# Attention, soft mixture and MLP in one kernel: keys and queries of most pairs loaded further ahead, one buffer cleared by VectorE, fewer filling products

## The chip, the cores and the metric

The kernel runs on one core of a Trainium2 chip (trn2). The metric is device time of one execution in microseconds (us): the median of the runs, which for the kernel before is 782.35 us.

## What is computed

Three stages in a row, all in float32 in the reference:

```python
q_pool = q.reshape(B, H, S // 2, 2, D).mean(axis=3)        # 4 x 8 x 576 x 64
scores = q_pool @ k.T / sqrt(D);  scores -= scores.max(-1)   # 576 queries x 1152 keys
x = softmax(scores) @ v                                      # then (B * 576) x 512 tokens
logits = x @ phi;  d = softmax over tokens;  slots = d.T @ x # 8 experts x 4 slots
slot_out[e] = relu(slots[e] @ w1[e]) @ w2[e]
x = softmax over slots (logits) @ slot_out
h = x @ w_in;  g = h where h >= 1, 0 where h <= -1, else (h + 1)^2 / 4
out = g @ w_out
```

q, k and v are 4 x 8 x 1152 x 64. The change touches the first stage alone, and the way the work is laid out there.

## The kernel before

**Pairs, steps, slots.** The 32 heads are taken as 16 pairs P = 0..15. The keys of a pair are cut into 9 chunks of 128, so a pair takes 9 steps, and step g = 9 P + c works on chunk c of pair P. A step has two slots h = 0, 1, one for each head. Below, (g, h) names a slot; negative steps are the start-up. In a slot TensorE computes, in this order: products whose maxima belong to a pair 11 steps ahead (`max_half`, L305; VectorE reduces them, L317), the transposed scores of this chunk (`st`, L371: four products with the keys K and then four with a second operand S, which hold the low parts of K and q and the subtracted maximum), and the products of the exponentials of the chunk before with V (`pv`, L401). ScalarE takes the exponential of the scores (L376), and VectorE adds exponentials for the denominators (L384). PSUM tiles of products and scores come from one pool of three buffers.

**Preparing a pair.** Keys and queries are split into two 16-bit floats (high and low part) and transposed by DMA. For pair P the steps are: load K and q (`load_k2`, L229, two DMAs; `load_q`, L237 to L240, four DMAs), high part of K on ScalarE (`prep_khi`, L252), low part on VectorE (`prep_klo`, L260), sum of neighbouring queries (`prep_qp`, L273), its high part (`prep_qhi`, L276), its low part (`prep_qlo`, L283), transposition of K in two halves (`xpose_k`, L266) and of the high part of q (`xpose_q1`, L288), a copy of the transposed q into the other 64 partitions (`dup_q1`, L291), and, when all maxima of the pair are there, `max_fin` with the transposition of the low part of q and the maxima (q2, L354). `s2_fill` (L294) copies K into S, `load_v` (L246) loads V.

**What sets the order.** The order is written out by hand. `at(g, h, f, ...)` puts a function into a slot, and `plan(P)` does so for a pair with offsets from the row of `PREP` (L44) that L587 picks: its entries are the step of the loads, of `prep_khi`, the half-steps of `prep_klo`, the half-step of `prep_qp`, the step of `prep_qhi` and the half-step of `prep_qlo`. Pair 2 takes the first row, pairs 3 to 15 the second. Pairs 0 and 1 are prepared by code of their own at the start, where POOL takes over some of the work for pair 1 (the scaling L679 among it). Each engine runs its instructions in program order. All DMAs are issued by SyncE's queue (SP), in program order too: a row that waits holds all rows behind it. The tiles `kf` and `qf` of the loads are single buffers, so the loads of a pair wait until `prep_klo` and `prep_qlo` of the pair before have read them.

**Between the loads** SP also issues rows of a background conversion: an output write (L209) and a load (L185) of weights.

**Start.** L663 to L665 clear the unused parts of qn2 and S, once for each of two buffers. `fill(FILL[2])` (L337) issues 128x128 products on the identity that nobody reads, 11 of them in slot (-3, 1); each is a float32 product and shows as two matrix rows.

**LGT** (L33) holds the half-steps at which the logits of a batch, and what follows from them, are put (`lg_part` to `p_add`).

Of the kernel before, what the change touches and what calls it, by code (L numbers as in the profile page):

```python
# [17 lines left out]


WARM = 2, 2, 3, 2, 4, 3  # L20
FILL = 28, 0, 11

AHEAD = 2
RUN = 3
# [5 lines left out]
P1G = -2, -1, 0, 1, 2, 3, 4, 5, 6  # L30
TMUL = (12, 0, 0, (0, 1)), (12, 1, 0, (2,)), (12, 1, 1, (0,)), (13, 0, 1, (1, 2))
TXN = 0, 1
LGT = 30, 31, 32, 33, 34, 36, 37  # L33
LPT = 6
WPH = 3
REA = 0
# [4 lines left out]
ADD = ((4, 1, 0, 0, 2), (5, 1, 1, 0, 1), (6, 1, 1, 1, 2), (6, 2, 0, 0, 2), (7, 2, 1, 0, 2), (8, 3, 0, 0, 1), (9, 3, 0, 1, 2),  # L41
       (10, 3, 1, 0, 2), (10, 4, 0, 0, 1), (11, 4, 0, 1, 2), (12, 4, 1, 0, 1), (13, 4, 1, 1, 2))

PREP = (-20, -18, (-34, -33), -36, -16, -30), (-24, -22, (-41, -37), -41, -19, -37)  # L44


@with_exitstack
def fused_kernel(ctx: ExitStack, tc: tile.TileContext, q, k, v, phi, w1, w2, w_in, w_out, out):
    nc = tc.nc
    B, H, S, D = q.shape  # L50
# [113 lines left out]
    S2b = [pr_p[i].tile([128, 2 * NK, 128], F16, name=f"S2_{i}") for i in range(2)]  # L164
    qn2b = [g2.tile([128, NK, 128], F16, name=f"qn2_{i}") for i in range(2)]
# [57 lines left out]
    def load_k(P, h):  # L223
        b, hp = divmod(P, HPB)
        if h == 0:

            kft[P] = g0.tile([128, 2, NK, D], F32, tag="kf", name=f"kf{P}") if P != 1 else \
                xT[:, 0:2].rearrange("p h (c d) -> p h c d", c=NK)
        nc.sync.dma_start(out=kft[P][:, h], in_=k[b, 2 * hp + h].rearrange("(p c) d -> p c d", p=128))  # L229
# [66 lines left out]
    def max_half(P, t, a):  # L296
# [10 lines left out]
        if P == 0:  # L307
            fill(FILL[1])
        rt = RT[P] if P < len(RT) else ()
# [23 lines left out]
    def fill(n):  # L333
        if not fl:
            fl[0] = acc_tile(0, "fill")
        for _ in range(n):
            nc.tensor.matmul(fl[0][:, 0:128], lhsT=ident, rhs=ident, start=True, stop=True)  # L337
# [243 lines left out]
    def at(g, slot, f, *a):  # L581
        sched.setdefault((g, slot), []).append((f, a))

    def plan(P):
        b = NK * P
        if P > 1:
            lk, hk, lok, aq, hq_, loq = PREP[P > 2]  # L587
            for h in range(2):
                at(b + lk, 0, (load_k2, load_q)[h], P)
                at(b + hk, h, prep_khi, P, h)  # L590
                at(b + lok[h] // 2, lok[h] % 2, prep_klo, P, h)
                at(b - 17, h, xpose_k, P, h)
            at(b + aq // 2, aq % 2, prep_qp, P)
            at(b + hq_, 0, prep_qhi, P)
            at(b - 16, 0, xpose_q1, P)
            at(b + loq // 2, loq % 2, prep_qlo, P)
            at(b - 15, 1, dup_q1, P)
        if P > 0:
            at(b - 8, 1, load_v, P)
            at(b - 9 if P > 1 else 1, 1, s2_fill, P)  # L600
        for s, *a in ADD:
            at(b + s // 2, s % 2, es_add, P, *a)
        for h in range(2):
            at(b + 9, h, tail_raw, P, h)
            if h and P:
                at(b + 2, 0, tail_fin, P - 1)
            at(b + 9, h, tail_sum, P, h)
        for c, i, ns in TAT:
            pre[b + c, i] = P, ns
        last = P == NP - 1  # L610
        if not last:
            at(b + 11, REA, tail_rec, P)
        for i in range(2):
            at(b + (10 if last else 12), i if last else TXN[i], tail_xn, P, i)
            if last:
                at(b + 12, i, tail_mul, P, i)
        if not last:
            for c, sl, *a in TMUL:
                at(b + c, sl, tail_mul, P, *a)
        if last:  # L620
            at(b + 11, 0, tail_rec, P)
            at(b + 11, 0, tail_fin, P)
        at(b + 13 + (not last), last, tail_xt, P)
        if P % HPB == HPB - 1:
            q_ = P // HPB
            if last:
                at(b + LPT, 1, lg_part, q_)
                at(b + 11, 1, lg_half, q_)
                at(b + 14, 1, lg_sum, q_)
                at(b + 14, 1, warm, WARM[0])  # L630
                at(b + 14, 1, raw_mm, range(B - 1))
                at(b + 14, 1, warm, WARM[5])
                at(b + 15, 1, lg_max, q_)
                at(b + 15, 1, lg_exp, q_)
                at(b + 15, 1, lg_raw, q_)
                at(b + 16, 1, lg_nat, q_)
                at(b + 16, 1, warm, WARM[1])
                at(b + 18, 1, raw_mm, (B - 1,))
                at(b + 18, 1, warm, WARM[2])
                at(b + 17, 0, p_mm, q_)  # L640
                at(b + 17, 0, p_add, q_)
            else:
                for f, t in zip((lg_part, lg_sum, lg_max, lg_exp, lg_nat, p_mm, p_add), LGT):
                    at(b + t // 2, t % 2, f, q_)
# [9 lines left out]
    with tc.manual_schedule():  # L654
# [4 lines left out]
        load_k(1, 1)  # L659
        fill(FILL[0])  # L660
        for i in range(2):
            eng = nc.gpsimd if i else nc.vector
            eng.memset(qn2b[i][:, :, D:2 * D], 0.0)  # L663
            eng.memset(S2b[i][64:128], 0.0)
            nc.gpsimd.memset(S2b[i][64:65], MS)  # L665
        prep_khi(0, 0)
        prep_klo(0, 0)
# [18 lines left out]
        for (g, i), *f in R1:  # L686
            for x in f:
                at(g, i, *x)
        at(-3, 1, fill, FILL[2])
        at(-3, 1, prep_qlo, 1)  # L690
        at(-2, 1, cv_load, 0)
        at(-2, 1, cv_load, 1)
        at(-2, 1, cv_load, 2)
# [1 line left out]
        for P in range(NP):  # L695
            plan(P)
# [8 lines left out]
        for g in range(-LEAD, nsteps + 1):  # L705
            mx = [divmod(g + LEAD, NK)] if not NK <= g + LEAD < 2 * NK else []
            mx += [(1, t) for t in range(NK) if P1G[t] == g]
            P, c = divmod(g, NK)
# [425 lines left out]
```

## Time and profile before

| what | value |
|---|---|
| median of 3 runs | 782.35 us (782.05 to 782.71) |
| profiled execution, its own time | 787.7 us |
| its span | 785.9 us |
| mean granted TensorE clock | 0.983 of full |
| TensorE (PE) busy | 757.1 us, 96% |
| VectorE (DVE) busy | 581.4 us, 74% |
| ScalarE (ACT) busy | 451.7 us, 57% |
| GpSimd (POOL) busy | 125.9 us, 16% |

The span runs from the first to the last instruction of the profiled execution. Busy time is the union of an engine's instructions. A share of 96% on PE is an average over stages: the start-up and a few places behind it are where PE stands still or runs at half clock. "Granted clock" is the share of TensorE's full clock that the chip lets through; 1.00 is 2.4 GHz and 0.50 is 1.2 GHz.

### The profile page before, as it was taken

What the parts mean: (1) busy time and instruction counts of PE and PEld (TensorE: products, weight loads), DVE (VectorE), ACT (ScalarE), POOL (GpSimd) and SP (SyncE); (2) the same over time, 40 slices, a digit from 0 to 9 for tenths busy, and PEclk for the clock granted to TensorE, in tenths of its full rate; (3) what the DMA queues carried; (4) which work ended last, traced back from release to release, by engine and by line L of the source; (5) the groups of instructions that cost most, each with busy time, mean ns of one, the idle gap of its engine ahead of it and who ended that gap; (6) DMA issues with size and microseconds to landing.
All of it is one profiled execution on the core that took longest, in us unless ns stands there. A gap on an engine that the chain in (4) does not pass through costs nothing.

```text
span 785.9 us, 19049 instructions
## 1 busy us (share of the span) xinstructions
PE 757.1 (96%) x7896; PEld 556.6 (71%) x7896; DVE 581.4 (74%) x947; ACT 451.7 (57%) x855; POOL 125.9 (16%) x100
## 2 busy tenths in 40 slices
PE   7779999999999999999999999999789999999998
PEld 6557777766767766777766776633578888888887
DVE  6878999988989888999988793151697777666520
ACT  4246667676657565676675666401686777556620
POOL 7000000000000000000000000002574444443330
PEclk8889999999999999999999999999989999999999
DMA  8786788797788797799998836799600000000000
GB/s 215 201 174 137 182 193 205 206 248 200 186 233 203 183 260 164 188 263 180 212 263 134 222 96 237 269 333 395 241 0 28 28 28 20 7 28 28 27 28 28
DMA packets 138263, 127.11 MB, mean 162 GB/s; under 512 B 80576, under 2 KB 100288, under 8 KB 137408
## 3 DMA queue, kind: packets, MB, share of 16 engines
q1 hardware_dynamic: 138176, 125.89, 61.0%
q8 instruction: 62, 1.02, 0.6%
q14 instruction: 25, 0.20, 0.1%
HBM read 87.10 MB, written 13.11 MB: 128 GB/s over the span
## 4 chain that ended last, share of the span: by engine, by line
PE 60%; DMA 2%; DVE 2%; ACT 2%; issue 1%; SPq 0%; ACTq 0%; DVEq 0%
PE acc L401 9%; PE st L371 9%; PE po L1031 8%; PE po L1032 8%; PE po L1033 8%; PE mx L305 4%; PE acc L394 3%; DMA wi<-wi_dr 2%; PE h L968 2%; PE h L775 2%; PE tx L439 1%; PE tb L466 1%; DVE r L1021 1%; PE tr L428 1%; PE lp L482 0%
## 5 line engine op out<-in xcount | busy, mean ns | idle before, releaser
L376 ACT ACTIVATE e<-st 128x576 f32<-128x576 f32 x288 | 187.0, 651 | 139.0 <-PE st L371 125.6
L317 DVE TENSOR_REDUCE mp<-mx 128x1 f32<-128x576 f32 x282 | 212.1, 754 | 44.9 <-PE mx L305 38.0
L401 PE MATMUL acc<-e,vf 128*64 128x288 f32 x1152 | 195.1, 411 | 0.5 <-ACT e L376 0.5
L305 PE MATMUL mx<-K,q 128*64 128x288 f16 x1152 | 124.8, 298 | 9.6 <-DVE mp L317 3.4
L371 PE MATMUL st<-q,K 128*64 128x288 f16 x1152 | 122.0, 288 | 5.9 <-ACT e L376 4.7
L371 PE MATMUL st<-q,S 128*64 128x288 f16 x1152 | 122.0, 287 | 0.0
L305 PEld LDWEIGHTS <-q 128*64 128x64 f16 x1152 | 66.3, 112 | 70.2 <-issue 24.5
L1031 PE MATMUL po<-whi,ghi 128*128 128x512 f32 (+1 forms) x280 | 108.5, 388 | 0.0
L1032 PE MATMUL po<-wlo,ghi 128*128 128x512 f32 (+1 forms) x280 | 108.5, 388 | 0.0
L1033 PE MATMUL po<-whi,glo 128*128 128x512 f32 (+1 forms) x280 | 108.0, 386 | 0.0
L981 DVE TENSOR_TENSOR r<-cl,r 128x1024 f32<-128x1024 f32 x34 | 80.6, 2372 | 36.9 <-ACT cl L980 36.9
L987 POOL TENSOR_TENSOR glo<-r,ghi 128x1024 fp32r<-128x1024 f32 x34 | 82.2, 2417 | 95.3 <-ACT ghi L986 95.3
L401 PEld LDWEIGHTS acc<-e,vf 128*64 128x64 f32 x1152 | 77.4, 137 | 8.3 <-ACT e L376 2.0
L371 PEld LDWEIGHTS <-K 128*64 128x64 f16 x1152 | 68.3, 110 | 20.9 <-issue 12.7
L752 POOL MEMSET xfer<- 128x1024 f32 x1 | 1.0, 957 | 493.5 <-PE pb L562 493.5
L384 DVE TENSOR_TENSOR es<-es,e 128x288 f32<-128x288 f32 (+1 forms) x144 | 77.5, 550 | 2.2 <-ACT e L376 2.2
L371 PEld LDWEIGHTS <-S 128*64 128x64 f16 x1152 | 69.3, 110 | 3.4
L971 ACT ACTIVATE r<-h,cols 128x512 f32<-128x512 f32 x68 | 43.0, 685 | 31.4 <-PE h L968 31.4
L1033 PEld LDWEIGHTS po<-whi,glo 128*128 128x128 f32 x280 | 53.2, 190 | 10.8
L1031 PEld LDWEIGHTS po<-whi,ghi 128*128 128x128 f32 x280 | 53.4, 191 | 9.8
L1032 PEld LDWEIGHTS po<-wlo,ghi 128*128 128x128 f32 x280 | 53.3, 190 | 9.3
L972 DVE TENSOR_SCALAR cl<-h 128x512 f32<-128x512 f32 x68 | 43.8, 685 | 15.8 <-ACT r L971 13.9
(191 smaller groups left out, 854.1 us busy)
## 6 DMA issues: line engine op xcount, KB each, us to landing
w<-in_moe_w_dram SPq DMA_DIRECT2D x31, 1024.0 KB, 7.9
vf<-in_v_dram SPq DMA_DIRECT2D x16, 576.0 KB, 6.1
kf<-in_k_dram SPq DMA_DIRECT2D x30, 288.0 KB, 4.1
f<-in_moe_w_out_dram SPq DMA_DIRECT2D x16, 512.0 KB, 5.1
f<-in_moe_w_in_dram SPq DMA_DIRECT2D x16, 512.0 KB, 5.5
qf<-in_q_dram SPq DMA_DIRECT2D x30, 256.0 KB, 4.9
S<-K SPq DMA_DIRECT2D x16, 288.0 KB, 5.6
out_dram<-ob SPq DMA_DIRECT2D x17, 256.0 KB, 2.0
```

Source lines behind the costliest of these rows:

```text
L305: nc.tensor.matmul(ps[p0:p1, i, 0:HQ], lhsT=q1[P][:, t, p0:p1], rhs=kk[:, j * HQ:(j + 1) * HQ], start=True, stop=True)
L317: nc.vector.tensor_reduce(out=mp[P][:, t, a:a + 1], in_=ps[:, :, 0:HQ], op=ALU.max, axis=AX.XY)
L371: nc.tensor.matmul(ps[c0:c0 + 64, i, 0:HQ], lhsT=kk[:, ci, c0:c0 + 64], rhs=f[:, sl[i]], start=first, stop=not first)
L376: nc.scalar.activation(out=e, in_=ps[:, :, 0:HQ], func=AF.Exp, scale=ESC)
L384: nc.vector.tensor_tensor(out=Es[P, n, h][:, i0:i1], in0=a[:, i0:i1], in1=b[:, i0:i1], op=ALU.add)
L401: nc.tensor.matmul(acc[P, i][h * 64:(h + 1) * 64, 0:HQ], lhsT=vt[P][:, h, c, :], rhs=E[P, c, h][:, i, :], start=(c == 0), stop=(c == NK - ...
L972: nc.vector.tensor_scalar(out=cl[:, a:b], in0=src, scalar1=-1.0, scalar2=1.0, op0=ALU.max, op1=ALU.min)
L981: nc.vector.tensor_tensor(out=r[:, sl], in0=cl[:, sl], in1=r[:, sl], op=ALU.add)
L987: nc.gpsimd.tensor_tensor(out=glo[n, qd][:, sl], in0=r[:, sl], in1=ghi[n, qd][:, sl].bitcast(F32), op=ALU.subtract)
L1031: nc.tensor.matmul(po, lhsT=ghi[n, qd][:, j, sl], rhs=whi[:, f, cs], start=(f == 0), stop=False)
L1032: nc.tensor.matmul(po, lhsT=ghi[n, qd][:, j, sl], rhs=wlo[:, f, cs], start=False, stop=False)
L1033: nc.tensor.matmul(po, lhsT=glo[n, qd][:, j, sl], rhs=whi[:, f, cs], start=False, stop=(f == 15))
```

## The change

- `FILL[2]` goes from 11 to 3: 6 matrix rows in place of 22.
- The clearing of the second S buffer (64 partitions of S) moves from POOL to VectorE, which clears it as 1152 elements of 32 bits instead of 2304 of 16.
- `prep_qlo(1)` moves from slot (-3, 1) to (-1, 1).
- The first row of `PREP` now holds for pairs 2 and 3, the second for pairs 4 to 15. Pair 3 so loads at step 7 instead of 3 and its four VectorE operations stand at half-steps 18, 20, 21 and 24 instead of 13, 13, 17 and 17.
- In the second row the loads come two steps earlier (-26 instead of -24).
- For pairs 4 to 15 the transpositions of K and q and the copy of q come one step earlier.
- The last three entries of `LGT` come one slot later (34, 36, 37 become 35, 37, 38).

```diff
--- before.py
+++ after.py
@@ -18,7 +18,7 @@
 
 
 WARM = 2, 2, 3, 2, 4, 3
-FILL = 28, 0, 11
+FILL = 28, 0, 3
 
 AHEAD = 2
 RUN = 3
@@ -30,7 +30,7 @@
 P1G = -2, -1, 0, 1, 2, 3, 4, 5, 6
 TMUL = (12, 0, 0, (0, 1)), (12, 1, 0, (2,)), (12, 1, 1, (0,)), (13, 0, 1, (1, 2))
 TXN = 0, 1
-LGT = 30, 31, 32, 33, 34, 36, 37
+LGT = 30, 31, 32, 33, 35, 37, 38
 LPT = 6
 WPH = 3
 REA = 0
@@ -41,7 +41,7 @@
 ADD = ((4, 1, 0, 0, 2), (5, 1, 1, 0, 1), (6, 1, 1, 1, 2), (6, 2, 0, 0, 2), (7, 2, 1, 0, 2), (8, 3, 0, 0, 1), (9, 3, 0, 1, 2),
        (10, 3, 1, 0, 2), (10, 4, 0, 0, 1), (11, 4, 0, 1, 2), (12, 4, 1, 0, 1), (13, 4, 1, 1, 2))
 
-PREP = (-20, -18, (-34, -33), -36, -16, -30), (-24, -22, (-41, -37), -41, -19, -37)
+PREP = (-20, -18, (-34, -33), -36, -16, -30), (-26, -22, (-41, -37), -41, -19, -37)
 
 
 @with_exitstack
@@ -584,17 +584,17 @@
     def plan(P):
         b = NK * P
         if P > 1:
-            lk, hk, lok, aq, hq_, loq = PREP[P > 2]
+            lk, hk, lok, aq, hq_, loq = PREP[P > 3]
             for h in range(2):
                 at(b + lk, 0, (load_k2, load_q)[h], P)
                 at(b + hk, h, prep_khi, P, h)
                 at(b + lok[h] // 2, lok[h] % 2, prep_klo, P, h)
-                at(b - 17, h, xpose_k, P, h)
+                at(b - 17 - (P > 3), h, xpose_k, P, h)
             at(b + aq // 2, aq % 2, prep_qp, P)
             at(b + hq_, 0, prep_qhi, P)
-            at(b - 16, 0, xpose_q1, P)
+            at(b - 16 - (P > 3), 0, xpose_q1, P)
             at(b + loq // 2, loq % 2, prep_qlo, P)
-            at(b - 15, 1, dup_q1, P)
+            at(b - 15 - (P > 3), 1, dup_q1, P)
         if P > 0:
             at(b - 8, 1, load_v, P)
             at(b - 9 if P > 1 else 1, 1, s2_fill, P)
@@ -659,9 +659,8 @@
         load_k(1, 1)
         fill(FILL[0])
         for i in range(2):
-            eng = nc.gpsimd if i else nc.vector
-            eng.memset(qn2b[i][:, :, D:2 * D], 0.0)
-            eng.memset(S2b[i][64:128], 0.0)
+            (nc.gpsimd if i else nc.vector).memset(qn2b[i][:, :, D:2 * D], 0.0)
+            nc.vector.memset(S2b[i][64:128], 0.0)
             nc.gpsimd.memset(S2b[i][64:65], MS)
         prep_khi(0, 0)
         prep_klo(0, 0)
@@ -687,7 +686,7 @@
             for x in f:
                 at(g, i, *x)
         at(-3, 1, fill, FILL[2])
-        at(-3, 1, prep_qlo, 1)
+        at(-1, 1, prep_qlo, 1)
         at(-2, 1, cv_load, 0)
         at(-2, 1, cv_load, 1)
         at(-2, 1, cv_load, 2)
```

**SP between the transposition of pair 2's K and pair 1's q2.** K1_P, q1_P and q2_P are the transposed tiles of pair P, kfP and qfP its loads, phs is the weight phi. Before:

```order
L288 DMA_TRANSPOSE q1_2_478<-qn1_105 128x9x128
L229 DMA kf3_523<-in_k_dram 128x576 x2
L237 DMA qf3_526<-in_q_dram 128x4x128
L238 DMA qf3_526<-in_q_dram 128x4x128
L239 DMA qf3_526<-in_q_dram 64x128
L240 DMA qf3_526<-in_q_dram 64x128
L291 DMA q1_2_478<-q1_2_478 64x1152
L694 DMA phs_100<-in_moe_phi_dram 128x4x32
L354 DMA_TRANSPOSE q2_1_666<-qn2_1_104 128x9x128
```

After the change:

```order
L288 DMA_TRANSPOSE q1_2_470<-qn1_105 128x9x128
L291 DMA q1_2_470<-q1_2_470 64x1152
L693 DMA phs_100<-in_moe_phi_dram 128x4x32
L354 DMA_TRANSPOSE q2_1_647<-qn2_1_104 128x9x128
L229 DMA kf3_709<-in_k_dram 128x576 x2
L237 DMA qf3_712<-in_q_dram 128x4x128
L238 DMA qf3_712<-in_q_dram 128x4x128
L239 DMA qf3_712<-in_q_dram 64x128
L240 DMA qf3_712<-in_q_dram 64x128
```

The loads of pair 3 now stand behind the copy of q1_2, the load of phi and the transposition of q2_1, where they stood ahead of them.

**SP around the transposition of pair 3's q.** vf2 is V of pair 2; wo_dr and f64 are the background conversion. Before:

```order
L266 DMA_TRANSPOSE K1_3_881<-kn3_614 128x9x128
L246 DMA vf2_904<-in_v_dram 128x2x576
L266 DMA_TRANSPOSE K1_3_881<-kn3_614 128x9x128
L209 DMA wo_dr_74<-wst1_797 128x512
L185 DMA f64_4_909<-in_moe2_w_out_dram 128x1024
L288 DMA_TRANSPOSE q1_3_939<-qn1_105 128x9x128
L229 DMA kf4_991<-in_k_dram 128x576 x2
L237 DMA qf4_994<-in_q_dram 128x4x128
L238 DMA qf4_994<-in_q_dram 128x4x128
L239 DMA qf4_994<-in_q_dram 64x128
L240 DMA qf4_994<-in_q_dram 64x128
L291 DMA q1_3_939<-q1_3_939 64x1152
```

After the change:

```order
L266 DMA_TRANSPOSE K1_3_870<-kn3_821 128x9x128
L229 DMA kf4_872<-in_k_dram 128x576 x2
L237 DMA qf4_875<-in_q_dram 128x4x128
L238 DMA qf4_875<-in_q_dram 128x4x128
L239 DMA qf4_875<-in_q_dram 64x128
L240 DMA qf4_875<-in_q_dram 64x128
L246 DMA vf2_901<-in_v_dram 128x2x576
L266 DMA_TRANSPOSE K1_3_870<-kn3_821 128x9x128
L209 DMA wo_dr_74<-wst1_781 128x512
L185 DMA f64_4_907<-in_moe2_w_out_dram 128x1024
L288 DMA_TRANSPOSE q1_3_938<-qn1_105 128x9x128
L291 DMA q1_3_938<-q1_3_938 64x1152
```

The six loads of pair 4 now stand ahead of the second half of K1_3 and of the transposition of q1_3, which they followed.

**VectorE in step 12, where the low part of pair 3's q now stands** (es0 and es1 are sums of exponentials, mp2 the maxima of pair 2). After the change:

```order
L317 TENSOR_REDUCE mp2_665<-mx2_5_0_961 128x1
L384 TENSOR_TENSOR es1_0_1_959<-e1_0_1_840,e1_1_1_896 128x288
L384 TENSOR_TENSOR es1_0_0_932<-es1_0_0_932,e1_2_0_924 128x576
L283 SCALAR_TENSOR_TENSOR qn2_1_104<-qf3_712,qn1_105 128x9x64
L317 TENSOR_REDUCE mp2_665<-mx2_5_1_993 128x1
L384 TENSOR_TENSOR es1_0_1_959<-es1_0_1_959,e1_2_1_955 128x576
```

L283 for pair 3, which reads qf3, stood in step 8, and now stands behind the sums of step 12; the loads of qf4 into the same buffer wait for it.

## Rows read from the trace of the kernel before

**Rows 1.** Windows: stretch, its length, busy us (instructions) of PE, PEld, DVE, ACT, POOL, granted clock, DMA share, GB/s.

```profile
22.60:29.00 6.40, 5.59 (x29) 4.72 (x27) 5.14 (x12) 0.00 (x0) 0.00 (x0) 0.50 0.52 99
53.00:59.60 6.60, 5.57 (x40) 3.56 (x41) 3.89 (x8) 2.90 (x5) 0.00 (x0) 0.50 0.35 67
```

**Rows 2.** Timeline of the start: start us, us, engine, line, operation, [idle before, releaser].

```profile
1.44 1.02 DVE L664 MEMSET S<- 64x1152 uint32 x1 [0.28 <-issue]
...
4.08 0.91 SPq L229 DMA_DIRECT2D xT<-in_k_dram  x2
4.57 0.76 DVE L260 SCALAR_TENSOR_TENSOR kn<-kf,kn 128x576 f16<-128x576 f32 x1 [2.11 <-ACT kn L252]
...
7.37 2.01 POOL L665 MEMSET S<- 1x2304 f16 x1
7.60 1.96 DVE L280 COPY qn<-qn 128x576 f16<-128x576 f16 x1 [0.75 <-ACT qn L276]
...
9.47 3.99 POOL L679 TENSOR_SCALAR xT<-xT 128x576 f32<-128x576 f32 x2
...
12.88 5.22 PE L305 MATMUL mx<-K,q 128*64 128x288 f16 x40 [3.24 <-DMA q<-qn]
...
23.11 0.37 DVE L327 TENSOR_TENSOR xnr<-xnr 128x432 f16<-128x432 f16 x1
```

**Rows 3.** One tile's view, pair 1's key loads into xT (4.0 to 4.4).

```profile
DMA to landing us min/median/max: 3.6/3.6/3.6
```

**Rows 4.** Timeline, end of the start-up.

```profile
24.82 4.69 PE L337 MATMUL fill<-ident 128*128 128x128 f32 x22
27.05 1.29 SPq L354 DMA_TRANSPOSE q<-qn  x1
...
32.05 0.44 PE L371 MATMUL st<-q,K 128*64 128x288 f16 x4 [0.23 <-DVE mp L317]
```

**Rows 5.** DMA issues at 27 to 28: issue, bytes, us to landing.

```profile
q<-qn SPq DMA_TRANSPOSE x1, 3.2
```

**Rows 6.** Timeline, steps 6 and 7.

```profile
51.04 0.68 ACT L252 ACTIVATE kn<-kf 128x576 f16<-128x576 f32 x1 [3.07 <-DMA kf<-in_k_dram]
52.31 0.44 PE L371 MATMUL st<-q,K 128*64 128x288 f16 x4 [2.88 <-ACT e L376]
...
55.46 0.69 PE L371 MATMUL st<-q,K 128*64 128x288 f16 x4 [1.03 <-ACT e L376]
```

**Rows 7.** Timeline, steps 11 to 16: SP's queue, VectorE, the first product of pair 3.

```profile
71.56 0.54 SPq L246 DMA_DIRECT2D vf<-in_v_dram  x1
...
75.10 2.62 SPq L288 DMA_TRANSPOSE q<-qn  x1
...
75.77 0.75 DVE L384 TENSOR_TENSOR es<-es,e 128x576 f32<-128x576 f32 x1
...
78.86 0.43 SPq L237 DMA_DIRECT2D qf<-in_q_dram  x1
...
81.63 0.53 SPq L291 DMA_DIRECT2D q<-q  x1
...
86.34 0.41 PE L305 MATMUL mx<-K,q 128*64 128x288 f16 x4
```

**Rows 8.** DMA issues at 75 to 76.

```profile
q<-qn SPq DMA_TRANSPOSE x1, 6.3
```

**Rows 9.** Tile q over the whole span: the score products, and its DMAs from issue to landing.

```profile
L371 PE MATMUL st<-q,K x1152: 282/286/448, 32.1 to 500.2; 128*64 128x288 f16 x192
...
DMA to landing us min/median/max: 2.2/4.8/7.5
```

**Rows 10.** Timeline, first products of pairs 8 and 9.

```profile
231.35 0.44 PE L305 MATMUL mx<-K,q 128*64 128x288 f16 x4 [0.72 <-DMA q<-q]
...
261.06 0.44 PE L305 MATMUL mx<-K,q 128*64 128x288 f16 x4 [1.76 <-issue]
```


## The prediction

> **What bounds the kernel now.** I read the shares first: TensorE is busy for 96% of the span, so in the steady part there is nothing to win by moving loads. Then the granted clock over the span, which shows where PE is slow, then the idle time before PE's instructions, and there the releaser. In the stretches of [rows 1] PE is busy nearly throughout, yet at a granted clock of 0.50, which is its level of 1.2 GHz; both follow idle time of PE. The timelines then name five places that the change touches: the wait for the first transposed q [rows 2], the filling products [rows 4], the wait of pair 3's K [rows 6], the queue of SP in steps 10 to 13 [rows 7], and the first products of later pairs [rows 10]. All five are on the path: PE runs in order and has no work left elsewhere, so what PE waits there moves the end.
>
> All durations are from the profiled execution, whose own time, 787.7 us, is 5.35 us (0.7%) above the median of the runs, 782.35 us. I take differences from its rows and put them on the median.
>
> **A, the buffer cleared by VectorE: -1.5 us.** VectorE's copy of q's high part starts at 7.60 and takes 1.96, while a VectorE operation on 432 of such elements took 0.37 when POOL was idle; 576 elements would then take 0.5. The copy ends at 9.56, 0.18 behind the end of POOL's clearing at 7.37 + 2.01 = 9.38 [rows 2]. I read it as held by POOL. The transposition of q starts right behind it, and PE's first product waits 3.24 for that [rows 2]. One clearing of 2.01 leaves POOL's queue, so the last ends at about 7.37. VectorE pays 1.02 for it, in a gap of 2.11 ahead of its next operation [rows 2], thus nothing on the path. The copy would end at 7.60 + 0.5 = 8.1 instead of 9.56: -1.5. But POOL's next work, the scaling of pair 1's keys, takes 2.0 each and is ready when the load issued at 4.08 has landed, 3.6 later, at 7.7 [rows 2, 3]: 0.1 behind the copy's start. If it gets in first, the copy ends at about 9.8. Bounds: -1.6 (the copy as fast as the smaller one) to +0.3; I take -1.5, since by these rows the copy is first.
>
> The Trainium skill, page "SBUF — State Buffer", section "Who interferes with whom", says that VectorE and GpSimd share a pair of ports under an exclusive lock, which the one that issues first keeps for its whole instruction. The copy's row agrees with it; by this rule alone a margin of 0.1 us decides between -1.5 and +0.3.
>
> **B, fewer filling products: -2.0 us.** 22 rows take 4.69, from 24.82 to 29.51 [rows 4], so 6 take 1.3 and end at 26.1. The first maxima of pair 1 then start about 3 earlier, but the scores cannot: their second part needs q2 of pair 0, transposed from 27.05 and landed 3.2 later, at 30.25 [rows 4, 5]. The first scores start at 32.05 now [rows 4], and at about 30.05 then. The low part of pair 1's q, moved behind two pairs of maxima, is out of their way and not needed until pair 1's q2, many steps later: nothing. Bounds: -2.9 (if q2 lands sooner) to 0; and below.
>
> Against it speaks that PE is on its lower level here [rows 1], and that fill is work which keeps it busy. The Trainium skill, page "TensorE: Matmul & The Clock Gate", section "Part 1: The HAM clock gate", says that the default is throttled and that activity releases it; by that rule the cut could keep the clock low for longer. This is a rival below.
>
> **C, pair 3 loaded at step 7: -6.7 us.** ScalarE's K conversion waits 3.07 for the load of pair 3's keys, and holds the exponentials behind it; PE stands 2.88 and again 1.03 [rows 6], and then runs 6.60 at half clock, busy for 5.57 [rows 1], which at full clock would be half: 2.8. Sum 2.88 + 1.03 + 2.8 = 6.7. With the conversion at step 9, two steps behind the loads, the wait goes. What is late next: SP now issues the copy of q1_2 right behind its transposition, so it waits there for the landing and phi, q2_1 and the loads queue behind it; the copy itself is not later than before. I allow up to 1.0 given back.
>
> **D, SP's queue in steps 10 to 13: +9.5 us.** This is the new wait. Pair 4's loads stand at step 10, ahead of the second half of pair 3's K and of the transposition of q1_3. The q loads wait until VectorE has done L283 for pair 3, which is in step 12 now, as the order shows. VectorE's sum there runs from 75.77 to 76.5 [rows 7]; two operations of 0.67 from start to start were added ahead of it (the low part of K and the sum of q, which were earlier in the program), and L283 itself is another: 78.5. Then four q loads, which take 81.63 - 78.86 = 2.8, and what lies between vf2 and the transposition, 75.10 - 71.56 = 3.5: the transposition starts at about 84.8 instead of 75.10 [rows 7]. The copy waits for its landing, 6.3 then [rows 8], or 3.2 on a quieter queue [rows 5], and lands 2.2 to 4.8 after its own issue [rows 9]. So the copy is there between 90.2 and 95.9. The first product of pair 3 starts at 86.34 [rows 7], with VectorE's lag of about 0.5 at 86.85. PE stands between 3.3 and 9.0; I take the middle, 6.2. Then it falls to the lower level as in C: 2.8. With the 0.5 of lag this is 9.5. Bounds: 1.9 (the shortest, with VectorE 1.5 us ahead and no fall of the clock) to 12.3. It happens once: from pair 4 on, low parts are early again and the loads wait for nothing.
>
> **E, later pairs one step earlier: -2.5 us.** The first products of pairs 8 and 9 wait 0.72 and 1.76 for the copy of q [rows 10]. 288 slots lie between 32.1 and 500.2 [rows 9], 1.63 each; the copy is two slots or 3.3 earlier, more than either wait: -2.5. Loads two steps earlier and LGT one slot later I cost at nothing: PE is busy around them; without that cover each of three LGT entries would move by a slot, once for a batch. Bounds: -3.0 to -1.0.
>
> Sum: -1.5 - 2.0 - 6.7 + 9.5 - 2.5 = -3.2, so **779.2 us** (782.35 - 3.2).
>
> **The rivals.**
> - *D is light.* SP has slack that I do not see, or transposition and copy land at the short end. For it speaks 3.2 for q2 [rows 5]; against it 6.3 for this very tile [rows 8]. With D between 1.9 and 4.3: 771.6 to 774.0 us.
> - *A and B are lost.* POOL's scaling gets in first and the clock stays low through the first steps. A becomes +0.3; B loses its 2.0, and up to 2 more at the lower level. Sum 0.3 + 0 - 6.7 + 9.5 - 2.5 = +0.6, up to +2.6: 783.0 to 785.0. For it speaks the margin of 0.1; against it that maxima follow the fill at once, so PE is not idle.
> - *Slower: the copies of q come late in every later pair.* In the new order a conversion write, its load and a V load stand ahead of the copy from pair 4 on; they took 75.10 - 71.56 = 3.5 with half a K transposition [rows 7]. Where the copy is issued 3.3 earlier this only cancels, but where the write waits for VectorE, the copy is later than before. It decides where the landing passes the pair's first product; pair 9 is past that point by 1.76 already [rows 10]. If each of 12 pairs waits 1.0, it is +12 in place of E's -2.5; A to D give -1.5 - 2.0 - 6.7 + 9.5 = -0.7, and 782.35 - 0.7 + 12 = 793.7. Against it: only two of these pairs wait at all now.
> - *D is heavy* (12.3) and A is lost: 0.3 - 2.0 - 6.7 + 12.3 - 2.5 = +1.4, 783.8.
>
> **How the numbers follow.** Forecast 0.52 (its own range 776 to 781.5), D light 0.21, A and B lost 0.12, late copies 0.07, D heavy 0.08. A measurement of this kernel tells about 0.2% from no change, so faster is below 780.8 and slower above 783.9. Faster: 0.21 and most of 0.52, 0.70. Same: the upper end of the forecast and half of the two middle rivals, 0.16. Slower: the rest, 0.14. The range goes from the light D with a little more, 771.0, to the heavy one, 784.0; the late copies and the tails of the others, under 2 in 10, are outside.
>
> **What would show it.** A: the copy L280 takes about 0.5 and PE's first product starts at about 11.2. B: the filling takes 1.3 and the first scores start 2.0 earlier relative to the first product. C: ScalarE's L252 for pair 3 waits for no load, and the clock stays at 1.00 through steps 6 to 8. D: L237 for pair 4 waits on VectorE, the transposition of q1_3 is issued some 9 us later against its step, and the first product of pair 3 waits for a DMA of q. If it does not, the time is near 770 and D is wrong. E: no idle time ahead of the first products of pairs 8 and 9. A wait for q in many later pairs would make the forecast wrong on the other side.

## The result, and the profile after

The changed kernel takes 788.35 us (median of 13 runs, 783.05 to 791.72), the kernel before 782.52 us (13 runs beside them). The ratio is 1.0071, 95% interval 1.0051 to 1.0092: slower by 0.7%, or 5.8 us. The forecast was 779.2 us, and the time lies above its range.

| profiled execution | before | after |
|---|---|---|
| own time, span | 787.7, 785.9 us | 791.72, 789.9 us |
| mean granted clock | 0.983 | 0.984 |
| PE, DVE, ACT, POOL busy | 757.1, 581.4, 451.7, 125.9 us | 757.4, 581.2, 450.9, 123.3 us |

Busy times hardly differ, so the time went into waits. I went through the start of each slot's first score product (L371) in both traces; a jump of the difference names the place. The first scores come 3.7 us earlier, and 3.5 of that is lost by step 2. From step 5 to 7 the changed kernel gains 6.3. From step 11 to 16 it loses 9.7. Steps 61, 70 and 78 together gain 4.1, step 97 loses 3.8. Around steps 46, 82 and 118, where the moved entries of LGT fall, it loses 0.3 each time. The last scores come 4.2 later.

**The start.** Timeline of the kernel after (start us, us, engine, line, operation, [idle before, releaser]):

```profile
7.82 0.33 DVE L280 COPY qn<-qn 128x576 f16<-128x576 f16 x1 [0.75 <-ACT qn L276]
...
9.13 3.93 POOL L678 TENSOR_SCALAR xT<-xT 128x576 f32<-128x576 f32 x2 [1.83 <-DMA xT<-in_k_dram]
...
11.94 0.93 PE L305 MATMUL mx<-K,q 128*64 128x288 f16 x12 [1.15 <-DMA q<-qn]
...
23.90 1.65 PE L337 MATMUL fill<-ident 128*128 128x128 f32 x6
...
28.35 0.44 PE L371 MATMUL st<-q,K 128*64 128x288 f16 x4
...
33.99 0.76 DVE L273 TENSOR_TENSOR qf<-qf 128x576 f32<-128x576 f32 x1 [3.69 <-DMA qf<-in_q_dram]
...
35.47 0.69 PE L371 MATMUL st<-q,K 128*64 128x288 f16 x4 [1.36 <-DVE mp L317]
```

The copy takes 0.33 and is ahead of POOL; the first product comes 0.9 earlier than in [rows 2], the first scores 3.7 earlier than in [rows 4]. But VectorE then stands 3.69 at L273, the sum of pair 2's queries, for the load of qf2. It holds the maxima behind it, and PE waits for those. The granted clock falls to 0.50. Windows of the kernel after (columns as in [rows 1]):

```profile
32.00:34.00 2.00, 1.50 (x16) 1.00 (x16) 0.01 (x1) 1.42 (x3) 0.00 (x0) 1.00 1.02 288
34.00:38.00 4.00, 2.64 (x20) 2.01 (x19) 4.00 (x6) 0.65 (x1) 0.00 (x0) 0.60 0.78 298
50.00:60.00 10.00, 9.93 (x160) 7.31 (x159) 7.42 (x15) 5.04 (x8) 0.00 (x0) 1.00 0.61 153
...
90.00:92.00 2.00, 2.00 (x44) 1.48 (x36) 0.00 (x0) 0.02 (x1) 0.00 (x0) 0.50 0.00 0
```

The third row answers to the second of [rows 1]: around step 7 PE is busy for 9.93 of 10 us at full clock. The wait of [rows 6] is gone. The fourth lies behind the wait in step 16, which is told next.

**Steps 10 to 16.** Timeline of the kernel after:

```profile
66.33 0.81 SPq L229 DMA_DIRECT2D kf<-in_k_dram  x2
...
71.17 0.75 DVE L283 SCALAR_TENSOR_TENSOR qn<-qf,qn 128x576 f16<-128x576 f32 x1
...
71.94 0.38 SPq L237 DMA_DIRECT2D qf<-in_q_dram  x1
...
74.75 1.32 SPq L266 DMA_TRANSPOSE K<-kn  x1
...
77.73 1.69 SPq L288 DMA_TRANSPOSE q<-qn  x1
...
80.27 0.68 ACT L252 ACTIVATE kn<-kf 128x576 f16<-128x576 f32 x1 [1.76 <-DMA K<-kn]
...
85.16 0.50 SPq L291 DMA_DIRECT2D q<-q  x1
...
87.63 0.69 PE L305 MATMUL mx<-K,q 128*64 128x288 f16 x4 [4.17 <-issue]
```

SP stands from 67.1 to 71.9 at the load of qf4 and goes on right behind L283. The second half of K1_3, V and the transposition of q1_3 wait behind it. The transposition lands 7.4 later, then the copy is issued, and PE's first product of pair 3 comes 2.5 behind that, after 4.17 of idle time. A second wait shows at 80.27: ScalarE's conversion for pair 4 needs the buffer kn, which the late transposition of K1_3 still reads.

**Step 97.** Timeline of the kernel after, and then its DMA issues at 346.6 to 347.1:

```profile
344.18 1.60 SPq L185 DMA_DIRECT2D f<-in_moe_w_in_dram  x1
346.21 0.38 SPq L246 DMA_DIRECT2D vf<-in_v_dram  x1
346.64 0.51 SPq L291 DMA_DIRECT2D q<-q  x1
...
354.36 0.44 PE L305 MATMUL mx<-K,q 128*64 128x288 f16 x4 [1.97 <-issue]
```

```profile
q<-q SPq DMA_DIRECT2D x1, 144.0 KB, 7.6
```

The copy of pair 12's q follows 512 KB of conversion and 576 KB of V at once, and lands 7.6 after its issue, when PE already waits. In the first profile of before it landed 3.6 after its issue. Behind the wait PE runs at half clock again; a window:

```profile
355.80:359.00 3.20, 3.20 (x46) 1.98 (x40) 0.39 (x1) 0.22 (x1) 0.00 (x0) 0.50 0.78 76
```

### The profile page after: what moved, and what is told of

The parts are those of the page before. It is cut to its first block, busy times and chain, and to the rows that moved or that the text cites. A ratio compares the mean times of both kernels' runs of the same rounds, so it can differ in the third digit from the quotient of the medians.

```text
span 789.9 us, 19046 instructions
## 1 busy us (share of the span) xinstructions
PE 757.4 (96%) x7880; PEld 554.9 (70%) x7880; DVE 581.2 (74%) x948; ACT 450.9 (57%) x855; POOL 123.3 (16%) x99
## 4 chain that ended last, share of the span: by engine, by line
PE 83%; DMA 5%; DVE 4%; ACT 3%; issue 2%; POOL 2%; SPq 1%; ACTq 0%; DVEq 0%; POOLq 0%
PE st L371 18%; PE acc L401 17%; PE mx L305 9%; PE po L1032 7%; PE po L1030 7%; PE po L1031 7%; PE acc L394 6%; DMA wi<-wi_dr 2%; PE h L774 2%; PE tx L439 2%; PE h L967 2%; DVE mp L317 2%; DMA q<-qn 1%; PE tb L466 1%; ACT e L376 1%
## 5 line engine op out<-in xcount | busy, mean ns | idle before, releaser
L371 PE MATMUL st<-q,K 128*64 128x288 f16 x1152 | 122.7, 289 | 4.5 <-ACT e L376 1.8
L371 PE MATMUL st<-q,S 128*64 128x288 f16 x1152 | 122.5, 287 | 0.6 <-DMA q<-qn 0.6
L371 PEld LDWEIGHTS <-K 128*64 128x64 f16 x1152 | 68.9, 110 | 20.6 <-issue 12.9
L384 DVE TENSOR_TENSOR es<-es,e 128x288 f32<-128x288 f32 (+1 forms) x144 | 77.4, 549 | 2.2 <-ACT e L376 2.2
L371 PEld LDWEIGHTS <-S 128*64 128x64 f16 x1152 | 69.8, 110 | 4.2 <-issue 0.8
```

The costliest lines, as they stand in the source:

```text
L371: nc.tensor.matmul(ps[c0:c0 + 64, i, 0:HQ], lhsT=kk[:, ci, c0:c0 + 64], rhs=f[:, sl[i]], start=first, stop=not first)
L384: nc.vector.tensor_tensor(out=Es[P, n, h][:, i0:i1], in0=a[:, i0:i1], in1=b[:, i0:i1], op=ALU.add)
```

## The experiments

Times are medians beside runs of the kernel before on the same chip (781.7 to 782.3 us in the three groups); a ratio, with its 95% interval, is to those. The runs of two kernels that were not in the same group are best compared by their ratios; where the medians give another difference, both are named.

**1. Pair 4 loaded late.** In the changed kernel:

```diff
             lk, hk, lok, aq, hq_, loq = PREP[P > 3]
+            lk += 2 * (P == 4)
```

> The changed kernel with pair 4 alone loaded at step 12 again, behind the transposition of q1_3, as before the change; nothing else differs. Theory (the queue of SP in steps 10 to 13 costs the changed kernel about 9.7 us, since the six loads wait for VectorE's L283 and hold the transposition of q1_3): the idle time of 4.17 us ahead of the first product of pair 3 goes, with the half clock behind it, and the time falls by 9 to 10 us, from 788.3 to about 778.6. Rival (the transposition and its copy land late anyway, since the queue is full there; or a wait for pair 4's keys takes the place): the time falls by less than 4 us, to 784.5 or more, and PE still stands in steps 15 to 17.

780.52 us, ratio 0.9970 (0.9959 to 0.9982): 7.8 us less than the changed kernel. The wait is gone. Timeline:

```profile
69.95 2.68 SPq L288 DMA_TRANSPOSE q<-qn  x1
...
72.02 0.75 DVE L283 SCALAR_TENSOR_TENSOR qn<-qf,qn 128x576 f16<-128x576 f32 x1
72.69 1.04 SPq L229 DMA_DIRECT2D kf<-in_k_dram  x2
...
76.44 0.48 SPq L291 DMA_DIRECT2D q<-q  x1
...
82.29 0.41 PE L305 MATMUL mx<-K,q 128*64 128x288 f16 x4
```

The transposition is issued 7.8 us earlier, ahead of L283, and PE's first product of pair 3 has no idle time ahead of it. The theory's size was 9 to 10; 7.8 by the medians (7.9 by the ratios) is less.

**2. Pair 3 alone, and pairs 3 and 4.** In the kernel before; the second line only in the second of the two:

```diff
-            lk, hk, lok, aq, hq_, loq = PREP[P > 2]
+            lk, hk, lok, aq, hq_, loq = PREP[P > 3]
+            lk -= 2 * (P == 4)
```

> The kernel before with one edit: pair 3 takes the first row of the offsets, so it loads at step 7. Pair 4 still loads at step 12. Theory (the wait of ScalarE for pair 3's keys cost 6.1 us with the half clock behind it, and nothing takes its place as long as pair 4's loads stay behind the transposition of q1_3): 782.5 - 6.1 = 776.4, between 775.5 and 778. Rival (four more operations of VectorE in steps 9 to 12, or late landings, give most of it back at the first product of pair 3): 779.5 to 782.5, with idle time of PE in step 16.

> The kernel before with pair 3 loaded at step 7 (measured alone: 780.3) and pair 4 loaded at step 10 instead of 12, nothing else. Theory (the pair 4 loads at step 10 wait for L283 of step 12 and hold the transposition of q1_3): 780.3 + 7.8 = 788.1, between 786.5 and 789.7, with PE standing about 4 us at the first product of pair 3 and the half clock behind it. Rival (the wait needs the denser queue that the other edits make): under 784.

Pair 3 alone: 780.25 us, ratio 0.9972 (0.9956 to 0.9988), thus 2.2 us by the ratio (0.9 to 3.4), 2.0 by the medians, instead of 6.1. The theory's size is refuted, and the rival's number came out. Its mechanism did so only in part: PE has no idle time in step 16 in that trace, but from slot (9,0) to (17,0) it takes 26.9 us where the kernel before takes 25.4 in both profiles, with no single idle time of PE above 0.3. So about 1.5 is given back there, in the steps where pair 3's VectorE work now stands; this work was not tried alone. Pairs 3 and 4: 788.23 us, ratio 1.0083 (1.0061 to 1.0106), so pair 4's loads at step 10 add 8.0 us by the medians, 8.7 by the ratios. Timeline of the second:

```profile
72.62 0.38 SPq L237 DMA_DIRECT2D qf<-in_q_dram  x1
...
78.34 1.45 SPq L288 DMA_TRANSPOSE q<-qn  x1
...
84.79 0.50 SPq L291 DMA_DIRECT2D q<-q  x1
...
87.26 0.44 PE L305 MATMUL mx<-K,q 128*64 128x288 f16 x4 [3.47 <-issue]
```

The same chain as in the changed kernel, at the same times within 1 us. These two lines alone reproduce the changed kernel's time; gains and losses of the rest about cancel.

**3. The kernel before once more,** to see why pair 3 was worth so little.

> The kernel before, unchanged, profiled a second time. Theory (the profiled execution that the forecast was worked out from, 787.7 us where the median is 782.4, met a wait for pair 3's keys that is mostly not there: pair 3 alone was worth 2.0 us and not 6.7): ScalarE's L252 for pair 3 waits less than 2 us in sum where it waited 5.0, PE's first scores of step 9 come 3 us or more earlier against step 5 than the 17.3 us of the first profile, and the execution takes 780 to 784 us. Rival (the wait is in every execution and something else gives the gain back): 5.0 us of waiting again, and again some 17 us from step 5 to step 9.

781.52 us, a single run. Timeline, and a window:

```profile
50.19 0.68 ACT L252 ACTIVATE kn<-kf 128x576 f16<-128x576 f32 x1 [2.60 <-DMA kf<-in_k_dram]
51.44 0.68 ACT L252 ACTIVATE kn<-kf 128x576 f16<-128x576 f32 x1
51.46 0.69 PE L371 MATMUL st<-q,K 128*64 128x288 f16 x4 [2.41 <-ACT e L376]
```

```profile
51.30:54.50 3.20, 3.04 (x22) 2.48 (x23) 0.39 (x1) 1.44 (x3) 0.00 (x0) 0.50 0.63 150
```

The second conversion of pair 3's keys had waited as well in the first profile:

```profile
54.19 0.68 ACT L252 ACTIVATE kn<-kf 128x576 f16<-128x576 f32 x1 [1.93 <-DMA kf<-in_k_dram]
```

ScalarE waits once, 2.60, where it waited 3.07 [rows 6] and 1.93, and the stretch from slot (5,1) to (9,0) takes 14.8 us instead of 17.3. My numbers for the theory (under 2, and 3 or more) were missed by a little; the direction holds. PE's idle time fell from 2.88 and 1.03 to 2.41, and the half clock behind it covers 3.2 us here where it covered 6.6 [rows 1]. By the slots, the two executions of the same kernel differ by 5.8 at the last scores: 0.4 at the start, 2.6 in steps 6 and 7, and 0.8, 1.9 and 1.2 in steps 61, 70 and 78, less 1.3 in steps 97 and 106, where the second one waits. Those of steps 61 and 70 are the waits of [rows 10].

Four of the kernels below (4, 5, 8 and 9) also load pair 3 at step 3. PE waits for ScalarE there too, 1.7 to 1.9, and in three of them 0.7 to 0.9 more for the copy of q1_2; but the clock stays at 1.00 in all four, and the stretch from (5,1) to (9,0) takes 12.9 to 13.6. With pair 3 at step 7 and nothing else in the way it takes 11.0. So the wait is in all six traces of kernels that load pair 3 at step 3, and the half clock behind it in two. A window of 8:

```profile
49.00:60.00 11.00, 9.07 (x140) 6.75 (x141) 8.29 (x17) 6.23 (x11) 0.00 (x0) 1.00 0.50 125
```

**4. Later pairs alone.** In the kernel before (pair 3 is kept as it was):

```diff
-PREP = (...), (-24, -22, (-41, -37), -41, -19, -37)
+PREP = (...), (-26, -22, (-41, -37), -41, -19, -37)
+            lk += 2 * (P == 3)
-                at(b - 17, h, xpose_k, P, h)
+                at(b - 17 - (P > 3), h, xpose_k, P, h)
-            at(b - 16, 0, xpose_q1, P)
+            at(b - 16 - (P > 3), 0, xpose_q1, P)
-            at(b - 15, 1, dup_q1, P)
+            at(b - 15 - (P > 3), 1, dup_q1, P)
```

> The kernel before with the edits for later pairs alone: loads of pairs 4 to 15 two steps earlier, their transpositions and the copy of q one step earlier. Pair 3, the start and LGT are as before. Pair 4's loads wait for nothing here, since pair 3's low parts are early. Theory (the copies of q gain a step but now have a conversion load and V right ahead of them in the queue, so that single waits go and others come): no change within 1.5 us, 780.8 to 783.8, with the wait of 1.76 us in step 70 gone and one of about 2 us elsewhere, such as step 97. Rival, the forecast's own term: 2.5 us faster, 779.8.

783.79 us, ratio 1.0026 (1.0008 to 1.0044): 2.0 us slower (0.6 to 3.4), at the upper end of what the theory gave. The forecast's term has the wrong sign. Timeline and DMA issues (339.9 to 340.5):

```profile
83.53 0.44 PE L305 MATMUL mx<-K,q 128*64 128x288 f16 x4 [1.24 <-issue]
...
339.50 0.40 SPq L246 DMA_DIRECT2D vf<-in_v_dram  x1
339.95 0.68 SPq L291 DMA_DIRECT2D q<-q  x1
...
348.70 0.69 PE L305 MATMUL mx<-K,q 128*64 128x288 f16 x4 [2.95 <-issue]
```

```profile
q<-q SPq DMA_DIRECT2D x1, 144.0 KB, 8.7
```

The copy lands 8.7 after its issue, at 348.6, and PE then runs at half clock (0.50 from 348.5 to 351.7). In the second execution of before it was issued at 341.71, 1.8 later, and landed 4.1 after that, at 345.8; PE waited there too, but less (the row names ScalarE, whose work had ended at 345.4; the copy's landing is what comes last):

```profile
345.92 0.44 PE L305 MATMUL mx<-K,q 128*64 128x288 f16 x4 [0.71 <-ACT e L376]
```

The first line of the timeline above (83.53) is a second loss, in step 16: pair 4's loads, which wait for nothing here, still stand ahead of the transposition of q1_3. The copy is issued at 81.11 and lands at 83.44, and the stretch from slot (11,0) to (17,0) takes 20.7 us instead of 19.3. The waits of [rows 10] are gone, in this trace as in the six others with the earlier copies.

**5. Later pairs, with V behind the copy.** The kernel of 4 and:

```diff
-            at(b - 8, 1, load_v, P)
+            at(b - 8 + 2 * (P > 2), P <= 2, load_v, P)
```

> The kernel before with the edits for later pairs (measured alone: 2.0 us slower) and V of pairs 2 to 14 loaded behind the copy of q. Theory (the copies land late, 8.7 us after their issue before step 97, because a conversion load of 512 KB and V with 576 KB are issued right ahead of them): with V behind, the copy there lands within 6 us, the wait of 2.95 us in step 97 goes, and the time is 2 us or more below the 783.8 of the edits alone: 779.5 to 782. Rival (the conversion load alone, or the pace of SP, makes the copies late): 783 or more, with the wait in step 97 still over 2 us.

The edit moves V of pairs 3 to 15, where the text above names 2 to 14. 780.96 us, ratio 0.9991 (0.9978 to 1.0004). The wait in step 97 is gone, and with it the loss, though the copy still takes 7.0 (I had expected under 6): it goes out earlier, and that is just enough. Over pairs 4 to 15 the copies land 4.5 after their issue on average in the first profile of before, 6.8 in experiment 4 and 5.2 here. So V ahead of them accounts for most of the delay on average, but not for that of pair 12, behind the conversion's 512 KB. The wait in step 16 is still there, 1.15. Timeline:

```profile
338.16 0.34 SPq L185 DMA_DIRECT2D f<-in_moe_w_in_dram  x1
338.55 0.51 SPq L291 DMA_DIRECT2D q<-q  x1
339.31 0.38 SPq L246 DMA_DIRECT2D vf<-in_v_dram  x1
...
345.66 0.44 PE L305 MATMUL mx<-K,q 128*64 128x288 f16 x4
```

**6. The sum of pair 2's queries later.** In the changed kernel:

```diff
+            aq += 2 * (P == 2)
```

> The changed kernel with the sum of pair 2's queries (L273) one step later on VectorE, at half-step 2 instead of 0; nothing else differs. Theory (the 2.0 us that the shorter fill gained are lost again because VectorE stands 3.7 us at L273 for the load of qf2 and holds the maxima behind it, until PE stands too and falls to half clock): PE loses less than 1 us between slots (0,0) and (2,0) where it lost 3.5, and the time falls by 1.5 to 3.5 us, to 784.8 to 786.8. Rival (six filling rows are too few, the clock falls whatever VectorE does): a granted clock of 0.50 around 34 to 38 us as before and no change, 788.3. The wait of pair 3 in steps 10 to 16 is left in.

784.96 us, ratio 1.0035 (1.0016 to 1.0053), 3.4 us below the changed kernel by the medians, 2.8 by the ratios, as the theory had it. L273 still waits, 1.43, but with less behind it, and the clock does not fall:

```profile
34.00:38.00 4.00, 3.47 (x44) 2.57 (x42) 3.91 (x6) 1.92 (x4) 0.00 (x0) 1.00 1.13 296
```

This row is the window that had 0.60 and 2.64 in the changed kernel; PE is busy for 3.47 now. At 50 us PE waits 1.19 for a sum of VectorE (L384), which gives some of it back.

**7. The filling back.** In the changed kernel:

```diff
-FILL = 28, 0, 3
+FILL = 28, 0, 11
```

> The changed kernel with the 22 filling rows back; nothing else differs. Theory (the wait of VectorE for qf2, not the fill, sets where step 2 starts): the first scores start about 2 us later than in the changed kernel, the wait at L273 gets shorter by as much, and step 2 starts about where it does now: 787.3 to 788.8, no change within 1 us. Rival (the clock wants the fill): the 3.5 us that the changed kernel loses between slots (0,0) and (2,0) are not lost, and the time falls by 1.5 to 3.5 us.

787.43 us (5 runs, 786.67 to 791.59), ratio 1.0070 (1.0045 to 1.0094): no change against the changed kernel, as the theory had it, though with intervals of about 2 us either way a difference of 1 or 2 us would not show. The first scores start 2.4 later in its trace, but step 2 starts 1.2 earlier, not at the same time, and the clock stays at 1.00 there. So the trace leaves something to the rival.

**8. The filling alone.** In the kernel before: `FILL` with 3, and `prep_qlo(1)` in slot (-1, 1).

> The kernel before with 6 filling rows instead of 22 and pair 1's low part behind two pairs of maxima, nothing else. Theory (scores start 2 us earlier, and VectorE's wait for qf2 at L273 takes it back, with the fall of the clock behind it): 782 to 784, no gain. The forecast's own term: 2.0 us faster, 780.3. A rival (the clock falls for longer): 785 or more.

780.51 us, ratio 0.9985 (0.9971 to 0.9999): a gain of 1.2 us (0.1 to 2.3), between the theory and the forecast's term. Timeline and window:

```profile
34.59 0.76 DVE L273 TENSOR_TENSOR qf<-qf 128x576 f32<-128x576 f32 x1 [3.99 <-DMA qf<-in_q_dram]
...
36.07 0.44 PE L371 MATMUL st<-q,K 128*64 128x288 f16 x4 [1.81 <-DVE mp L317]
```

```profile
32.00:36.00 4.00, 1.60 (x16) 0.99 (x16) 1.41 (x3) 1.58 (x3) 0.00 (x0) 1.00 1.05 334
```

VectorE waits as long as in the changed kernel and takes the 2 us back: slot (2,0) starts at 37.5, in the two profiles of before at 38.0 and 37.6. Where the gain of 1.2 comes from this trace does not show. The clock stays at 1.00 here. Why it falls in one and not in the other these runs do not settle.

**9. The buffer alone.** In the kernel before: the second S buffer cleared by VectorE.

> The kernel before with one edit: VectorE clears the second S buffer. Theory (the copy L280 is no longer held by POOL, and everything behind it comes 1.5 us earlier, with no wait behind it that takes it back): the first product at about 11.3 us instead of 12.9, and 782.3 - 1.5 = 780.8, between 780.2 and 781.5. Rival (the load of qf2 sets step 2, and it is issued behind q2 of pair 0, which comes earlier by as much as the rest: no loss; or a wait behind it takes it back): 782.3, no change.

780.95 us, ratio 0.9999 (0.9985 to 1.0013): inconclusive, since the interval holds both no change and a gain of 1.2 us; the 1.5 of the forecast lies just outside. In its trace the copy takes 0.33 and the first product starts at 11.81, 1.1 earlier.

**10. Three repairs together.** The changed kernel with the edits of 1, 5 and 6.

> The changed kernel with pair 4's loads at step 12, pair 2's sum of queries one step later on VectorE, and V of pairs 2 to 14 loaded behind the copy of q instead of ahead of it. Theory (the three waits are independent): 788.3 - 7.8 (pair 4, measured) - 3.4 (the sum, measured) = 777.1, and 0 to 2 us less for the copies of q: 775 to 777.5, faster than both kernels. Rival (the waits overlap, so that taking one away uncovers another): 778.5 to 781.

777.28 us, ratio 0.9946 (0.9931 to 0.9961): faster than before by 4.2 us and than the changed kernel by 11.1. The three waits add up, as the theory had it. In its trace none of the three is left, and still the clock is at its lower level for a while behind the first scores, with L273 not in the way (it waits 0.75):

```profile
30.40:33.60 3.20, 3.20 (x27) 2.67 (x24) 1.46 (x3) 2.41 (x4) 0.00 (x0) 0.50 1.05 318
```

So VectorE's wait is not the only way to that fall. Between the first scores and step 4 the clock falls in three of the six traces with six filling rows (the changed kernel, 1 and 10) and in none of the eight with 22. Whether the short fill makes it likelier is open.

**11. Without the later pairs.** The kernel before with the buffer, the short fill with `prep_qlo(1)` moved, pair 3 in the first row, and pair 2's sum at half-step 2.

> The changed kernel without its edits for later pairs and for LGT, and with pair 2's sum of queries one step later: that is the kernel before with the buffer cleared by VectorE, the short fill, pair 3 at step 7 and the sum at half-step 2. Theory (what is left has no wait of its own): 782.2 - 2.0 (pair 3) - 1 to 1.5 (the buffer) - 0 to 2 (the fill without its wait) = 776.7 to 779.2. Rival (the edits for later pairs with V behind the copy are what brought the 777.3 of the version with three repairs): 779.5 or more.

777.93 us, ratio 0.9947 (0.9930 to 0.9964). The same gain, within the intervals, without any edit to later pairs. What pays here is the start and pair 3. In this trace PE still waits 0.83 and 1.65 at the places of [rows 10], and in that of 10 it does not; 10 in turn pays the 1.0 of LGT (below). The kernel of 10 without the edit of LGT was not run.

## Why the prediction was wrong

The parts measured alone, beside the forecast's terms:

| part | forecast | measured | from |
|---|---|---|---|
| A, buffer | -1.5 | -0.1 (-1.2 to +1.0) | 9 |
| B, fill | -2.0 | -1.2 (-2.3 to -0.1) | 8 |
| C, pair 3 | -6.7 | -2.2 (-3.4 to -0.9) | 2 |
| D, SP's queue | +9.5 | +8.7 | 2 (7.9 by 1) |
| E, later pairs | -2.5 | +2.0 (0.6 to 3.4) | 4 |
| sum | -3.2 | +7.2 | the change: +5.8 |

The measured column is ratio less 1, times 782; D is the difference of two ratios. Pair 4's loads ahead of q1_3 are in the runs of D and of E, so some 1.4 (experiment 4, step 16) is counted twice. LGT was not tried alone, but the traces show it: over steps 44 to 48, 80 to 84 and 116 to 120 together the five traces with that edit take 57.2 us and the nine without it 56.2, each to 0.02. The forecast put it at nothing; it costs 1.0. With both, the parts give 6.8, which agrees with the measured 5.8 (4.0 to 7.2). Of the 10.4 us between the two sums, 4.5 are C's and 4.5 are E's.

**C failed in its size.** The step "sum 2.88 + 1.03 + 2.8 = 6.7" took its durations from one execution, 5.35 us above the median, and put the difference on the median as it was. That excess was named and then not looked for. It lay in steps 6 and 7 and in later waits: experiment 3 shows 2.6 of it in steps 6 and 7, and the edit alone is worth 2.2. The term that was mis-sized most is the half clock, 2.8: it is absent in four of the five other traces with pair 3 at step 3. And about 1.5 is given back from (9,0) to (17,0), where the forecast allowed up to 1.0 and left it out of the sum. The mechanism was right: after the change L252 for pair 3 waits for no load, and the clock is 1.00 there.

**E failed in its sign.** The step "the copy is two slots earlier, more than either wait" looked at when the copy is issued. What it gains was priced well. The waits at pairs 8 and 9 are gone in all seven traces with the earlier copies, and over the stretches around steps 61, 70, 78 and 106 the seven without them lose 0.5 to 4.1, 2.1 on average. What failed is that nothing new was priced against it. The copy's landing moved: behind 1.1 MB of conversion and V it took 7.6 and 8.7 in place of 3.6 and 4.1, and the forecast kept the old landing. Step 97 so loses up to 4.6 (experiment 4), and step 16 another 1.4. This is near the rival on late copies, at one pair instead of twelve; that rival had the copy issued late, while here it is issued earlier and lands late. It got a chance of 0.07.

**D was right,** in place, order and nearly in size: L237 behind L283, the transposition at 77.73, which with the 6.0 us that this execution was ahead by step 11 is 83.7 against a forecast 84.8, and the product of pair 3 waiting. The idle time was 4.17 instead of 6.2, with 1.17 more from ScalarE's wait for kn, which the forecast did not name. The half clock behind it came too (0.50 in the window at 90).

**A and B were right in mechanism** as far as the first scores, 3.7 earlier (forecast 3.5); against the second profile of before, whose first scores start at 30.90, it is 2.55. The copy got in ahead of POOL's scaling, by more than the 0.1 of the forecast: POOL waits for the load of pair 1's keys until 9.13, 1.0 behind the copy's end. POOL runs nothing while the copy does, so that who would win is not tried here. The Trainium skill, page "SBUF — State Buffer", section "Who interferes with whom", has the one that issues first keep the shared ports; 0.33 without work on POOL against 1.96 behind its clearing agrees with it. What was missed is what is late next: VectorE's wait at L273 for qf2, issued behind q2 of pair 0. In the first profile of before it is already there with 1.58, and the forecast never named it:

```profile
34.91 0.76 DVE L273 TENSOR_TENSOR qf<-qf 128x576 f32<-128x576 f32 x1 [1.58 <-DMA qf<-in_q_dram]
```

The rival in which the clock stays low through the first steps is refuted as stated: it was 1.00 at 32 to 34 us with six filling rows, and fell during PE's wait for VectorE. The later fall in three of six traces is not settled (experiment 10). The Trainium skill, page "TensorE: Matmul & The Clock Gate", section "Part 1: The HAM clock gate", has activity release the clock; the traces agree as far as they go: around the first scores the clock rose no later with six filling rows, between 26.1 and 29.1 us, than with 22, between 26.6 and 29.6.

## What to carry to other kernels

Where the profiled execution is slower than the median, find the excess before pricing a wait by it: waits for DMAs are the first suspects, and a second profile of the same kernel tells. The half clock behind a wait is a term of its own, which can be missing in the next execution. A load moved earlier is priced by the queue: what it waits for, who stands behind it, and which bytes now go ahead of a small transfer that somebody needs. Move a load only past rows that are later than its own wait; here one exception (pair 4 not among the early ones) turns a loss of 5.8 us into a gain of 1.7, by the medians.

## What was not expected

Executions of one kernel on one core differ by over 5 us (the kernel before 779.4 to 785.2 over all groups), and by the two traces compared nearly all of it lies at four places where PE waits, directly or through ScalarE, for a DMA, with the half clock behind one of them. A copy of 144 KB lands between 2.3 and 8.7 us after its issue: 2.4 with no other DMA under way (pair 3 after the change), 8.7 behind 1.1 MB.
